# Letting ScalarE issue some of the loads of a gated linear attention kernel, with a new order of all its steps

## The chip, the cores and the metric

The kernel runs on one NeuronCore of a Trainium2 chip. The core has five engines, each with its own queue of instructions that it works through in order: TensorE (PE, matrix products), VectorE (DVE), ScalarE (ACT), GpSimd (POOL) and SyncE (SP, which here only issues DMA transfers). Sixteen DMA engines move data between the device's memory and the core. The engines meet only through semaphores. The metric is the device time of one execution in microseconds (us).

## The reference

Gated linear attention for 4 batches, 8 heads, 768 tokens and 48 features a head, then a feed-forward layer with the greatest of three projections. In the reference's words, cut to what matters:

```python
state = np.zeros((B, H, D, D))
for t in range(S):
    state = alpha[:, :, t, :, None] * state + np.einsum('bhd,bhe->bhde', k[:, :, t], v[:, :, t])
    y[:, :, t] = np.einsum('bhd,bhde->bhe', q[:, :, t], state)
x = y.transpose(0, 2, 1, 3).reshape(B * S, H * D)          # 3072 x 384
h = np.maximum(np.maximum(x @ w1, x @ w2), x @ w3)         # 3072 x 768
out = h @ w_out                                            # 3072 x 384
```

All arrays come and go as 32-bit floats; inside, the kernel uses 16-bit floats for what TensorE reads.

## The kernel before, in words

**Tiling.** The 768 tokens are cut into six chunks of 128. A *unit* u is one chunk of one batch: 24 units, numbered chunk by chunk, u = 4 x chunk + batch. Two units of one chunk make a *group* n (12 groups), for which alpha, q, k and v are loaded together. Each of the four tensors has four buffers for groups (`LOADED = 4`), so group n reuses the buffer of group n - 4 and must wait until its readers are through. The first four groups are loaded in two halves of 192 KB a tensor (each half is one unit), the others in one piece of 384 KB. The weights come in eight pieces between them.

**The steps of a unit**, with the engine and the line of the profile in brackets. `load` brings alpha, q, k, v (SP, line 304). `ln` takes the logarithm of alpha (ACT, 398), `totals` and `e` turn it into the decay over half a chunk (PE 408, ACT 414), `G` into the decay of a whole one (DVE 420). `cums` sums the logarithms over the tokens with a triangular matrix (PE 438); `ep` and `en` are its exponentials, up and down (ACT 443, 446); `q~` and `k~` are q and k scaled by them (DVE or POOL, 450), `v` is v scaled and rounded (POOL or ACT, 457, 460). `turn` transposes q~ and k~ by eight matmuls with an identity (PE 479) and `qkT` copies the result out of PSUM (DVE or ACT, 486); for eight of the late units a DMA transpose, `cross`, does both (SP, 469). `scores` multiplies them (PE 495), `LA` applies the causal mask on the way out (DVE 500), `outs` multiplies with v and with the state Z of the earlier chunks (PE 538, 541), `xb` brings the result to memory (ACT or DVE, 552, 554), `x turn` and `xT` transpose it (PE 568; DVE or ACT 573), or `cross x` does for three units (SP, 561). `sums`, `U` and `Z` carry the state to the next chunk (PE 600, DVE 607, POOL or DVE 613).

**The feed-forward layer.** max(x w1, x w2, x w3) is written as x w1 + max(relu(x (w2 - w1)), x (w3 - w1)). So `cast` rounds w1 and w_out (ACT 329), `sub` builds the two differences (DVE or POOL, 337), and `w1 turn`, `w1T`, `fold`, `w1o` multiply w1 by w_out once (PE 362, 379; ACT 368, 386). For one unit or two at a time, `grow` forms the two products (PE 638), `relu` (ACT 649) and `max` (DVE 654) combine them, `shrink` multiplies by w_out and adds x times w1o (PE 674), `ob` copies the result out (ACT or DVE, 689) and `store` writes it (ACT or SP, 694). 27 `zeros` matmuls without use (PE 582) keep TensorE occupied at the start. `clear` (POOL 345) zeroes the padding of buffers that are used again.

**What sets the order.** The 801 steps are built in a list, each with its readers and writers; then one loop issues them in the order of the tuple `ORDER`, on the engine that the dictionary `PICK` chooses from the step's options (the first where it names none), with the PSUM banks of the tuple `BANKS`. All three are written out by hand as numbers; nothing is decided at run time:

```python
for i in ORDER:
    how, _, run, deps, _, _ = self.steps[i]
    done.add(i)
    run(how[PICK.get(i, 0)][0])
```

The numbers in the options are the costs that a planner used and have no effect here. As every engine's queue is in order, a step that waits holds what stands behind it on its engine. In the built program all DMAs share eight completion counters in turn, whichever engine issues them, and an issue waits, where it must, until the earlier DMA on its counter has landed.

Before, all 64 loads, the eight pieces of weights, eleven DMA transposes and seven stores are issued by SP; ACT issues two constants and 18 stores.

Of the kernel before, what the change touches and what calls it, by code (L numbers as in the profile page):

```python
# [32 lines left out]


ORDER = (
# [44 lines left out]
)  # L80
BANKS = (
# [9 lines left out]
)  # L91
PICK = {
# [8 lines left out]
}  # L101

HARD, HARD_LOAD, HARD_LATE, LATE_FROM = 0.5, 1.8, 1.5, 3


def load_options(share, n):
    return [("SP", HARD, 0, HARD_LOAD * share, HARD_LATE * (n >= LATE_FROM))]  # L110


def weight_options(share, cast):
# [57 lines left out]
def kernel(  # L171
# [125 lines left out]
    def load(n):  # L297
        cb, g = divmod(n, B // UB)
        pieces = [(i * H, (i + 1) * H) for i in range(UB)] if n < HALF_LOADS else [(0, HG)]
        for lo, hi in pieces:  # L300
            for x in "akqv":
                t = ld[x][n % LOADED]
                plan.step(f"load {x} {n} {lo}", load_options((hi - lo) / HG, n), n,
                          lambda e, x=x, t=t, lo=lo, hi=hi: engines[e].dma_start(  # L304
                              t[:, lo:hi],
                              views[x][cb * P:(cb + 1) * P, g * HG + lo:g * HG + hi]),
                          writes=[(x, n % LOADED, h) for h in range(lo // H, hi // H)])
# [455 lines left out]
```

## Time and profile before

| | before |
|---|---|
| median of three runs | 155.6 us |
| runs | 155.11, 155.60, 156.13 us |
| span of the profiled execution | 466.5 us |
| busy in it: PE, DVE, ACT, POOL | 457.5, 112.5, 90.1, 48.0 us |
| first matmul starts | 4.32 us |
| last issue, a store by SP | 463.93 us |
| moved: read, written | 23.69 MB, 4.72 MB |

The profiled execution took three times as long as the timed runs, and has to be read with that in mind: TensorE's matmuls in it are slow, the other engines wait for them, and so its idle times, its chain of waits and the moments at which things happen after the first few microseconds are not those of the timed runs. The durations of single instructions on the other engines, the sizes of transfers and the order of instructions are what can be used.

In a row of the view of groups stand line, engine, operation, output and input with partitions and elements, the count, busy time in all (us), the mean of one (ns), and the idle time of the engine before them with what ended it. In a timeline row the first number is the start, the second the duration; engines with a q (SPq, ACTq) are DMA issues on that engine's queue.

### The profile page before, as it was taken

Reading aid. Unit: us, or ns where it says so; the run is one execution under the profiler, and the core shown is the slowest. Engines: PE = TensorE matmul, PEld = TensorE weight load, DVE = VectorE, ACT = ScalarE, POOL = GpSimd, SP = SyncE. Lnnn points to the kernel's source line nnn. Section 1 sums busy time; section 2 is a strip of 40 time slices with the busy share of each in tenths; the row PEclk is TensorE's granted clock in tenths of the full one; section 3 lists DMA queues with packets and bytes.
Section 4 is the critical chain, followed back from the end, with each engine's and each line's share of the span. In section 5 each row is a group of like instructions: output and inputs, shape, how many; then the busy total and the mean of one; then the engine's idle time right before and its main releaser. Section 6 shows DMA issues by size and latency. Waiting matters only on the chain.

```text
span 466.5 us, 4171 instructions
## 1 busy us (share of the span) xinstructions
PE 457.5 (98%) x1683; PEld 263.5 (56%) x1683; DVE 112.5 (24%) x196; ACT 90.1 (19%) x177; POOL 48.0 (10%) x72
## 2 busy tenths in 40 slices
PE   4999999999999999999999999999999999999997
PEld 1667556674555656547546645545546554567473
DVE  5420313131123122222412221322221321231100
ACT  4323221122121312111212200121220111001010
POOL 0110002003001030210111120011110020000000
DMA  9999500540087000700032640020550030100001
GB/s 179 272 287 209 110 0 1 111 76 1 0 163 124 1 0 18 152 17 35 0 60 49 141 91 9 2 62 0 112 112 17 18 79 25 35 0 25 1 34 34
DMA packets 116131, 31.07 MB, mean 67 GB/s; under 512 B 109712, under 2 KB 114960, under 8 KB 116112
## 3 DMA queue, kind: packets, MB, share of 16 engines
q1 hardware_dynamic: 113232, 27.27, 27.9%
q10 hardware_dynamic: 2880, 3.54, 2.2%
q8 instruction: 13, 0.21, 0.2%
q14 instruction: 6, 0.05, 0.0%
HBM read 23.69 MB, written 4.72 MB: 61 GB/s over the span
## 4 chain that ended last, share of the span: by engine, by line
PE 98%; DMA 1%; SPq 0%; DVE 0%; issue 0%; DVEq 0%
PE psum L638 38%; PE psum L674 29%; PE psum L479 6%; PE psum L495 4%; PE psum L582 4%; PE psum L541 3%; PE psum L438 3%; PE psum L568 3%; PE psum L600 3%; PE psum L538 2%; PE psum L379 2%; DMA qn<-in_q_dram 1%; PE psum L362 1%; PE psum L408 1%; SPq L304 0%; DVE qk L450 0%
## 5 line engine op out<-in xcount | busy, mean ns | idle before, releaser
L638 PE MATMUL psum<-xT,wd 128*128 128x256 f16 (+1 forms) x540 | 186.4, 602 | 0.0
L638 PEld LDWEIGHTS <-wd 128*128 128x128 f16 x540 | 105.1, 209 | 67.5 <-issue 61.5
L674 PE MATMUL psum<-wo,hT 128*128 128x384 f16 (+1 forms) x150 | 96.7, 887 | 0.0
L674 PEld LDWEIGHTS <-hT 128*128 128x128 f16 x150 | 34.4, 230 | 54.6 <-issue 52.0
L674 PE MATMUL psum<-w1o,xT 128*128 128x384 f16 (+1 forms) x75 | 50.1, 847 | 0.0
L654 DVE TENSOR_TENSOR hT<-psum,hT 128x512 f16<-128x512 f32 (+1 forms) x39 | 24.7, 647 | 99.7 <-PE psum L638 99.7
L649 ACT ACTIVATE hT<-psum 128x512 f16<-128x512 f32 (+1 forms) x39 | 21.7, 564 | 111.0 <-PE psum L638 111.0
L500 DVE TENSOR_TENSOR LA<-psum,c 128x1024 f16<-128x1024 f32 x24 | 28.9, 1221 | 41.0 <-PE psum L495 28.7
L541 PE MATMUL psum<-v,LA 128*128 128x48 f16 x192 | 30.3, 314 | 0.0
L541 PEld LDWEIGHTS <-LA 128*128 128x128 f16 x192 | 26.5, 179 | 5.7 <-issue 5.1
L613 POOL TENSOR_TENSOR Z<-U,G 48x192 f16<-48x192 f32 x26 | 14.1, 543 | 109.5 <-DVE U L607 108.5
L438 PE MATMUL psum<-la,c 128*128 128x384 f16 x24 | 19.9, 847 | 4.3 <-ACT la L398 4.3
L479 PE MATMUL psum<-c,qk 128*128 128x128 f16 x96 | 22.1, 480 | 1.7 <-DVE qk L450 1.7
L479 PEld LDWEIGHTS <-qk 128*128 128x128 f16 x96 | 16.9, 208 | 9.1 <-DVE qk L450 4.0
L450 POOL TENSOR_TENSOR qk<-qn,ep 128x384 f16<-128x384 f32 x11 | 10.9, 994 | 105.2 <-ACT ep L443 94.0
L674 PEld LDWEIGHTS <-xT 128*128 128x128 f16 x75 | 13.1, 185 | 14.7 <-issue 14.2
L582 PE MATMUL psum<-Z 128*128 128x384 f16 x27 | 20.2, 869 | 0.0
L443 ACT ACTIVATE ep<-psum 128x384 f32<-128x384 f32 x24 | 11.7, 494 | 41.3 <-PE psum L438 41.2
L689 ACT COPY ob<-psum 128x384 f32<-128x384 f32 (+1 forms) x18 | 8.3, 469 | 54.7 <-PE psum L674 54.7
L554 DVE TENSOR_SCALAR xb<-psum,c 128x384 f16<-128x384 f32 x15 | 9.2, 617 | 37.9 <-PE psum L541 37.9
L568 PE MATMUL psum<-c,xb 128*128 128x128 f16 x63 | 17.5, 455 | 0.0
L446 ACT ACTIVATE en<-psum 128x384 f32<-128x384 f32 x24 | 11.5, 490 | 28.4 <-PE psum L438 27.1
(61 smaller groups left out, 297.2 us busy)
## 6 DMA issues: line engine op xcount, KB each, us to landing
out_dram<-ob ACTq DMA_DIRECT2D x17, 192.0 KB, 1.9
an<-in_alpha_dram SPq DMA_DIRECT2D x8, 384.0 KB, 5.3
kn<-in_k_dram SPq DMA_DIRECT2D x8, 384.0 KB, 5.4
qn<-in_q_dram SPq DMA_DIRECT2D x8, 384.0 KB, 5.7
vn<-in_v_dram SPq DMA_DIRECT2D x8, 384.0 KB, 4.2
ws<-in_moe_w_dram SPq DMA_DIRECT2D x3, 768.0 KB, 6.7
an<-in_alpha_dram SPq DMA_DIRECT2D x8, 192.0 KB, 4.0
kn<-in_k_dram SPq DMA_DIRECT2D x8, 192.0 KB, 4.0
```

The costliest lines, as they stand in the source:

```text
L438: nc.tensor.matmul(live[Lk], tri, la[:, hs, :D], start=True, stop=True)
L479: nc.tensor.transpose(live[tk][:, w, j, :], qk[:, w, 2 * j:2 * j + 2, :], ident)
L495: nc.tensor.matmul(live[Ak][:, p, j * P:(j + 1) * P], qkT[rows, 1, j, :], qkT[rows, 0, j, :], start=True, stop=True)
L500: lambda e: nc.vector.tensor_mul(LA.rearrange("p a b t -> p (a b) t"), live[Ak].rearrange("p a (b t) -> p (a b) t", t=P), maskA.unsqueeze( ...
L541: nc.tensor.matmul(yp[:, 2 * j + p, :], LA[:, p, j, :], v16[:, 2 * j + p, :], start=(cb == 0), stop=True, skip_group_check=True)
L568: nc.tensor.transpose(live[xk][:, ft, :], xb[:, ft * P:(ft + 1) * P], ident)
L582: nc.tensor.matmul(live["wm"], zero[:, :P], zero, start=True, stop=True)
L613: lambda e, rows=rows, cols=cols: engines[e].tensor_mul(Zn[rows, :, cols], (Us[u % 3] if cb else live[pk])[rows, :, cols], G[rows, i * NP: ...
L638: nc.tensor.matmul(live[gk][:, jj, :], wd[:, kt, g, j * P:(j + 1) * P], xT[:, kt, :], start=(kt == 0), stop=(kt == NFT - 1))
L649: lambda e, h=h, gk=gk: nc.scalar.activation(out=h, in_=live[gk], func=AFT.Relu),
L654: lambda e, h=h, gk=gk: nc.vector.tensor_max(h, live[gk], h),
L674: nc.tensor.matmul(live[ok][:, cols], a[:, i * P:(i + 1) * P], w[:, cols], start=(kt == 0), stop=(kt == nk - 1))
```

## The change

`load_options` gets a second option, ACT, and the three tables of numbers are new. The core of the diff:

```diff
 def load_options(share, n):
-    return [("SP", HARD, 0, HARD_LOAD * share, HARD_LATE * (n >= LATE_FROM))]
+    return [("SP", HARD, 0, HARD_LOAD * share, HARD_LATE * (n >= LATE_FROM)), ("ACT", 0.45, 0, HARD_LOAD * share)]
 ORDER = (
-    4, 5, 6, 0, 8, 9, 65, 2, 82, 1, 83, 84, 85, 10, 86, 64, 34, 88, 123, 3, 92, 89, 68, 7, 127,
...
+    0, 14, 12, 8, 5, 4, 123, 2, 64, 124, 13, 6, 1, 125, 9, 34, 3, 10, 65, 66, 82, 68, 127, 84,
...
 PICK = {
-    44: 1, 71: 1, 72: 1, 75: 1, 79: 1, 81: 1, 85: 1, 86: 1, 120: 1, 131: 1, 132: 1, 145: 1, 146:
...
+    2: 1, 17: 1, 18: 1, 19: 1, 20: 1, 23: 1, 27: 1, 29: 1, 31: 1, 45: 1, 81: 1, 122: 1, 130: 1,
...
```

The steps and their number are the same, 1683 matmuls among them. What the tables make of them, step by step with the engine that runs it:

| step | before | after |
|---|---|---|
| load | SP 64 | SP 41, ACT 23 |
| q~ and k~ | DVE 25, POOL 23 | DVE 17, POOL 31 |
| v | POOL 14, ACT 10 | POOL 13, ACT 11 |
| qkT | DVE 9, ACT 7 | DVE 15, ACT 1 |
| xb | DVE 15, ACT 9 | DVE 9, ACT 15 |
| xT | DVE 14, ACT 7 | DVE 6, ACT 15 |
| Z | POOL 26, DVE 14 | POOL 23, DVE 17 |
| ob | ACT 18, DVE 7 | ACT 12, DVE 13 |
| store | ACT 18, SP 7 | ACT 17, SP 8 |

The 23 loads on ACT are eight of q, three of alpha, three of k and nine of v, spread from the eighth place of `ORDER` to the 681st; ten of them are among the first 45 DMAs. In the built program 20 of the 23 wait for an earlier DMA on their counter.

At the start the order of the loads is another. Before, SP issues alpha, k and q of unit 1, then alpha of unit 0 and unit 2, and so on; unit 1 is through first. After, SP issues alpha of unit 0, q and alpha of unit 3, alpha of unit 2, k and alpha of unit 1, then k of unit 3 and q of unit 1; q of unit 0 is issued by ACT. k~ and q~ of units 1 and 0 are on POOL instead of DVE. The last piece of weights comes after 15 loads instead of 16.

120 rows, old and new, of tables (BANKS, ORDER, PICK) are left out of this document.

## The prediction

> **What bounds the kernel now.** I read the page first: the span, the busy times, the DMA queues, the chain that ended last.
>
> ```profile
> span 466.5 us, 4171 instructions
> ...
> PE 457.5 (98%) x1683; PEld 263.5 (56%) x1683; DVE 112.5 (24%) x196; ACT 90.1 (19%) x177; POOL 48.0 (10%) x72
> ...
> q1 hardware_dynamic: 113232, 27.27, 27.9%
> q10 hardware_dynamic: 2880, 3.54, 2.2%
> ...
> PE 98%; DMA 1%; SPq 0%; DVE 0%; issue 0%; DVEq 0%
> ```
>
> The profiled execution is not an execution like the timed ones. Its span is 466.5 us, the timed median 155.6 us, and its TensorE alone is busy for 457.5 us. So in the timed runs TensorE went at least 457.5 / 155.6 = 2.9 times as fast. The timeline of PE shows the slow pace directly:
>
> ```profile
> 7.90 0.95 PE L582 MATMUL psum<-Z 128*128 128x384 f16 x1
> ...
> 8.53 1.58 PE L438 MATMUL psum<-la,c 128*128 128x384 f16 x2
> ```
>
> One matmul of 384 columns shows 0.95 us, two show 1.58, so the second came 0.63 us after the first. The Trainium skill ("TensorE: Matmul & The Clock Gate", section "What's actually happening") gives 2.4 GHz for a warm array, which would be 0.16 us for 384 columns; its caveat in "Seeing it yourself", a clock stuck at a quarter for 50 us and more, agrees with the 0.63 us here, although this profile puts the granted clock at 1.000. By that figure PE's work would be, as an estimate, 457.5 x 0.16 / 0.63 = 116 us of the 155.6.
>
> The chain of waits (98% PE) therefore says nothing of the timed runs. What does hold there is what the other engines did, as their instructions do not run on PE's clock: VectorE 112.5 us, ScalarE 90.1, GpSimd 48.0; and the DMA engines' packets, (27.9% + 2.2%) of 466.5 = 140.4 us. Set against 155.6 us, DMA is at 90%, VectorE at 72%, ScalarE at 58%. PE's own share there is not in the trace. So the kernel has no single bound that I can name: it is a weave of four, each waiting for the others a little. The table by stretches shows where DMA is full:
>
> ```profile
> 0.00:20.00 20.00, 13.99 (x77) 7.64 (x78) 10.86 (x30) 8.46 (x13) 2.35 (x7) 1.00 0.93 216
> 20.00:40.00 20.00, 20.00 (x79) 12.25 (x77) 5.06 (x6) 5.72 (x11) 2.63 (x2) 1.00 1.08 267
> ```
>
> The last two columns are the DMA engines' share and GB/s: from the start to 40 us they are saturated, from SyncE's queue almost alone, and a piece of 192 KB takes 196.6 / 267 = 0.74 us there.
>
> I make my sum in differences on the rows of the side engines and set it on the median of 155.6 (155.11 to 156.13); the 466.5 us cannot carry it. About 1% (1.6 us) is what a measurement of this kernel can tell from no change.
>
> **The change, part by part.** *Side engines.* The work is the same; the steps are picked anew. Rows for the steps that change sides, in the view of groups by shape:
>
> ```profile
> L450 DVE TENSOR_TENSOR qk<-kn,en 128x384 f16<-128x384 f32 x11 | 6.4, 598 | 11.6 <-ACT en L446 11.6
> L450 POOL TENSOR_TENSOR qk<-qn,ep 128x384 f16<-128x384 f32 x11 | 10.9, 994 | 105.2 <-ACT ep L443 94.0 <-DMA qn<-in_q_dram 11.1
> ...
> L486 ACT COPY qkT<-psum 128x1024 f16<-128x1024 f16 x5 | 5.1, 1012 | 14.3 <-PE psum L479 14.3
> L486 DVE COPY qkT<-psum 128x1024 f16<-128x1024 f16 x6 | 4.2, 692 | 30.6 <-PE psum L479 30.6
> ...
> L689 ACT COPY ob<-psum 128x384 f32<-128x384 f32 x17 | 8.0, 478 | 48.7 <-PE psum L674 48.7
> L689 DVE COPY ob<-psum 128x384 f32<-128x384 f32 x6 | 3.2, 555 | 16.8 <-PE psum L674 16.8
> ...
> L573 DVE COPY xT<-psum 128x384 f16<-128x384 f16 x14 | 4.8, 356 | 38.9 <-PE psum L568 38.8
> L573 ACT COPY xT<-psum 128x384 f16<-128x384 f16 x7 | 3.3, 477 | 23.7 <-PE psum L568 23.7
> ...
> L554 DVE TENSOR_SCALAR xb<-psum,c 128x384 f16<-128x384 f32 x15 | 9.2, 617 | 37.9 <-PE psum L541 37.9
> L552 ACT ACTIVATE xb<-psum,c 128x384 f16<-128x384 f32 x9 | 5.2, 581 | 53.3 <-PE psum L541 53.3
> ...
> L457 ACT ACTIVATE v<-vn,c 128x384 f16<-128x384 f32 x10 | 6.2, 617 | 0.7 <-DMA vn<-in_v_dram 0.7
> L613 DVE TENSOR_TENSOR Z<-U,G 48x192 f16<-48x192 f32 x6 | 3.0, 493 | 0.1
> L613 POOL TENSOR_TENSOR Z<-U,G 48x192 f16<-48x192 f32 x26 | 14.1, 543 | 109.5 <-DVE U L607 108.5
> ```
>
> VectorE gives eight of q~ and k~ to GpSimd (-8 x 0.598 = -4.8), takes six qkT (+6 x 0.692 = +4.2) and six ob (+6 x 0.555 = +3.3) from ScalarE, gives it eight xT (-8 x 0.356 = -2.8) and six xb (-6 x 0.617 = -3.7), and takes three Z (+1.5): -2.4 in all (by the unrounded products), so 110.1 us. ScalarE: -6 x 1.012 - 6 x 0.478 + 8 x 0.477 + 6 x 0.581 + 0.617 for one v = -1.0. GpSimd: +8 x 0.994 - 3 x 0.543 = +6.3, so 54.3: far below the others, no cost.
>
> *Twenty-three loads on ScalarE.* An issue is not counted as busy, but it holds the engine that makes it, and what is queued behind it: ep and en (line 443, 446), which q~ and k~ wait for, relu, which frees the bank that PE's grow fills, and xb, xT, which PE's next transposes and grows wait for. The price is not in the trace, as ScalarE issues only constants and stores there. From below, its stores; from above, SyncE's issues of these very loads (min/median/max ns):
>
> ```profile
> L694 ACTq DMA_DIRECT2D out_dram<-ob x18: 338/338/446, 129.1 to 463.2; - x18
> ```
>
> ```profile
> L304 SPq DMA_DIRECT2D an<-in_alpha_dram x16: 457/847/3164, 0.7 to 327.4; - x16
> L304 SPq DMA_DIRECT2D kn<-in_k_dram x16: 507/1300/2517, 1.3 to 329.8; - x16
> L304 SPq DMA_DIRECT2D qn<-in_q_dram x16: 646/1309/1673, 1.9 to 328.1; - x16
> L304 SPq DMA_DIRECT2D vn<-in_v_dram x16: 368/878/3893, 9.4 to 341.2; - x16
> ```
>
> Moved are 8 loads of q, 3 of alpha, 3 of k, 9 of v. At SyncE's medians they cost 8 x 1.309 + 3 x 0.847 + 3 x 1.300 + 9 x 0.878 = 24.8 us; at its shortest, 0.368, a load with nothing ahead of it, 8.5 us. ScalarE's queue is emptier than SyncE's, but the DMA engines behind both are the same, so I take the middle between that shortest one and the longest median: 0.84 us, 19.3 us in all. That a load is not always cheap even behind an idle queue, these two pairs show, a store and the load right behind it, in the timeline of SyncE:
>
> ```profile
> 86.19 0.36 SPq L694 DMA_DIRECT2D out_dram<-ob  x1
> 86.60 1.18 SPq L304 DMA_DIRECT2D qn<-in_q_dram  x1
> ...
> 276.81 0.36 SPq L694 DMA_DIRECT2D out_dram<-ob  x1
> 277.21 0.43 SPq L304 DMA_DIRECT2D vn<-in_v_dram  x1
> ```
>
> The same pair costs 0.43 or 1.18 us; no view says what else the DMA engines had at 86.6. A packet of PE's instructions would be such a thing, and then loads issued when one comes get the dear price.
>
> So ScalarE, issues included: before 90.1 + 18 x 0.338 = 96.2; after 96.2 - 1.0 - 0.3 (one store less) + 19.3 = 114.2. It passes VectorE's 112.5, which has been the busiest engine beside PE and stands for the pace that the side engines allow. I cost the change at that difference, 114.2 - 112.5 = +1.7 us. Below 112.5, that is below (112.5 - 94.9) / 23 = 0.77 us an issue, this term is nothing.
>
> *Start.* Before, the three loads of one unit come first:
>
> ```profile
> 3.74 0.52 ACT L398 ACTIVATE la<-an 128x384 f16<-128x384 f32 x1 [0.83 <-DMA an<-in_alpha_dram]
> 4.32 0.53 PE L438 MATMUL psum<-la,c 128*128 128x384 f16 x1 [4.32 <-ACT la L398]
> ...
> 6.53 1.69 PE L479 MATMUL psum<-c,qk 128*128 128x128 f16 x8 [1.69 <-DVE qk L450]
> 6.74 0.52 ACT L398 ACTIVATE la<-an 128x384 f16<-128x384 f32 x1 [0.99 <-DMA an<-in_alpha_dram]
> 7.61 0.52 ACT L398 ACTIVATE la<-an 128x384 f16<-128x384 f32 x1 [0.35 <-DMA an<-in_alpha_dram]
> ```
>
> The first, fourth and fifth load let ln start at 3.74, 6.74 and 7.61. Afterwards unit 1 needs the sixth load on SyncE (about 8.5) and its k~ and q~ stand on GpSimd, one after the other at 0.994: the first transposes come at about 8.5 + (6.53 - 3.74) + 2 x (0.994 - 0.598) = 12.1 instead of 6.53, 5.6 us later. I cost it at nothing: until the last weight is in, PE has little else to do, and that comes after 15 loads instead of 16, 0.74 us sooner. The cover ends where the last weight lands, at about 32 us (4.3 MB by 20 us, the other 3.4 at 267 GB/s). Without it the cost is up to 5.6 us, with it the gain up to 0.7.
>
> *Order and banks* of the rest: no row prices them. PE's matmuls are the same 1683. Sum: 155.6 + 1.7 = 157.3 us.
>
> **The rivals.** *Faster, 153.2 us:* the issues are cheap. At under (110.1 - 94.9) / 23 = 0.66 us ScalarE stays below VectorE's new 110.1, and VectorE's own -2.4 us shows. For it: ScalarE's stores never took over 0.446 us; against it, SyncE's medians.
>
> *No change, 155.6 us:* DMA sets the pace, and who issues does not matter. For it: 0.93 and 1.08 of the DMA engines in the first 40 us, from one queue. The Trainium skill ("DMA: Bandwidth & Descriptors", section "Issuing engines are not separate DMA queues") has that rule: transfers of all engines run on the same sixteen and interleave, and a second issuer only saves the time of issuing; those two shares agree, and by it the time would stay.
>
> *Much slower, 164.7 us:* ScalarE is held by completion counters. In the built programs the DMAs share eight counters in turn, and an issue waits until the DMA eight places earlier has landed; 20 of the 23 loads carry such a wait. Landings:
>
> ```profile
> kn<-in_k_dram SPq DMA_DIRECT2D x8, 384.0 KB, 5.4
> kn<-in_k_dram SPq DMA_DIRECT2D x8, 192.0 KB, 4.0
> ```
>
> Eight pieces at 0.74 are 5.9 us, barely over a landing, so in the saturated stretch the counters come free just as they are wanted. Ten of the loads stand among the first 45 DMAs; held by one delivery each, they add 10 x 0.74 = 7.4 to ScalarE: 121.6, +9.1. It decides once the holds exceed what the engine waits for anyway.
>
> **How the numbers follow.** Slower by dear issues 0.43, faster 0.25, no change 0.20, held 0.12. The first case reaches from 155.6 to 162.7 (the medians, 94.9 + 24.8 = 119.7, +7.2); about 0.06 of its chance lies within 1%. So faster by over 1%: 0.25; within: 0.20 + 0.06, say 0.27; slower: 0.48. The likeliest case gives 157.3. The range goes from 152.5, the faster rival with the 0.7 of the start (153.2 - 0.7), to 163.0, the dear end of the first case; it leaves out the held case and, for the unpriced order, some of both ends.
>
> **What would show it.** In the profile after: load issues on ScalarE's queue with a median near 0.84 us (under 0.66: the faster rival; waits on DMA landings just before them: the held one); ScalarE's busy time at about 89 (90.1 - 1.0) and VectorE's at 110; the first transposes at about 12.1 us. The forecast is wrong if the issues are dear and the time does not rise, as ScalarE then had the room, or if the time moves by more than the side engines' sums do, as then the new order did it.

## The result, and the profile after

| | before | after |
|---|---|---|
| median | 155.36 us (4 runs, 154.19 to 156.13) | 160.03 us (4 runs, 158.69 to 160.07) |
| ratio, 95% interval | 1 | 1.0304 (1.0240 to 1.0368) |

The change makes the kernel 3% slower. The ratios are those to the kernel before in runs beside it; here and below they leave disturbed runs out, so they need not be the quotients of the medians. The profiled execution of the kernel before ran its TensorE at a quarter of the pace of the timed runs, so nothing can be set beside it; the kernel before was therefore profiled once more (156.37 us), and "before" below is that execution.

> The kernel before once more, for a profile in which TensorE runs at its normal pace, so that it can be laid beside the profile after. Expected time about 155.4 us (median of the four runs so far). Theory 'start' (the 4.7 us between the kernels arise in the first 45 us): PE is idle less than the 15 us or so that it is idle there after, and from then on the two kernels take equally long. Theory 'weave' (the new order costs all along): PE's idle time in the first 45 us is about the same in both, and the difference builds up afterwards.

From the pages, first of before, then of after: the span, the engines' busy time, for after the two DMA queues, and the chain of waits by engine (SPq and ACTq are the issues on the queues of SyncE and ScalarE).

```profile
span 154.6 us, 4171 instructions
...
PE 135.8 (88%) x1683; PEld 105.9 (69%) x1683; DVE 108.7 (70%) x196; ACT 88.1 (57%) x177; POOL 48.5 (31%) x72
...
PE 48%; SPq 25%; DMA 20%; issue 3%; ACT 1%; DVE 1%; POOL 0%; DVEq 0%; POOLq 0%; ACTq 0%
```

```profile
span 158.2 us, 4150 instructions
...
PE 136.4 (86%) x1683; PEld 106.1 (67%) x1683; DVE 107.4 (68%) x189; ACT 86.9 (55%) x180; POOL 56.4 (36%) x76
...
q1 hardware_dynamic: 75120, 20.19, 62.5%
q10 hardware_dynamic: 40992, 10.62, 32.7%
...
PE 73%; DMA 10%; SPq 7%; DVE 4%; issue 2%; ACT 1%; ACTq 0%; DVEq 0%
```

TensorE is the busiest of the engines in both, at 135.8 and 136.4 us; what changed is its idle time, 154.6 - 135.8 = 18.8 us before and 158.2 - 136.4 = 21.8 after. Before, the chain of waits runs through TensorE for only 48% of the span and through SyncE's issues and transfers for 45%; after, for 73% and 17%. VectorE and ScalarE lost 1.3 and 1.2 us of work, and no gain in time shows. Where the idle time lies, the table by stretches tells. It gives for PE, PEld (TensorE's loading of weights), DVE, ACT and POOL the busy time and the number of instructions, then the granted clock (the share of its full clock that TensorE was given), the DMA engines' share, and GB/s. Before:

```profile
0.00:10.00 10.00, 3.51 (x21) 1.61 (x21) 5.21 (x24) 5.36 (x10) 0.20 (x4) 1.00 0.87 172
10.00:20.00 10.00, 7.57 (x75) 5.13 (x76) 6.26 (x8) 3.50 (x4) 2.14 (x3) 1.00 0.90 236
20.00:30.00 10.00, 9.23 (x114) 7.17 (x112) 3.66 (x6) 7.57 (x15) 2.60 (x2) 1.00 1.08 330
30.00:40.00 10.00, 9.48 (x129) 7.46 (x128) 8.73 (x14) 6.74 (x17) 2.45 (x4) 1.00 1.00 208
```

After:

```profile
0.00:10.00 10.00, 1.22 (x18) 0.87 (x19) 3.37 (x20) 3.21 (x5) 0.20 (x4) 1.00 0.91 180
10.00:20.00 10.00, 8.22 (x62) 4.52 (x60) 4.31 (x6) 5.57 (x12) 5.44 (x6) 1.00 1.05 256
20.00:30.00 10.00, 7.33 (x106) 5.01 (x104) 6.85 (x8) 5.22 (x9) 4.24 (x3) 1.00 1.10 347
30.00:40.00 10.00, 6.39 (x48) 5.20 (x48) 2.63 (x2) 3.62 (x7) 0.56 (x2) 0.66 0.91 175
```

By 40 us TensorE has done 21 + 75 + 114 + 129 = 339 matmuls before, but 18 + 62 + 106 + 48 = 234 after, with 29.8 and 23.2 us of work: 6.6 us more idle time. Only 3.0 us of that is left at the end, so after 40 us TensorE idles 3.6 us less than before. That the new order is the better one there is not shown: the loads can have got ahead while TensorE stood still, and without the pause that follows here the new order is no faster than the old (`late_ln` below). The last stretch also shows a granted clock of 0.66. What happened between 22 and 40 us, the timeline of after shows (start, duration, what; in brackets the idle time before it and what ended it):

```profile
22.31 0.39 ACTq L304 DMA_DIRECT2D an<-in_alpha_dram  x1
...
26.06 0.80 ACT L368 COPY w1T<-psum 128x768 f16<-128x768 f16 x1
...
27.50 1.18 PE L638 MATMUL psum<-xT,wd 128*128 128x128 f16 x18 [0.46 <-POOL wd L337]
...
30.93 2.63 DVE L337 TENSOR_TENSOR wd<-ws,w1h 128x1536 f16<-128x1536 f32 x2 [2.63 <-DMA ws<-in_moe_w_dram]
...
32.67 0.52 ACT L398 ACTIVATE la<-an 128x384 f16<-128x384 f32 x1 [5.81 <-DMA an<-in_alpha_dram]
...
33.10 0.46 ACT L573 COPY xT<-psum 128x384 f16<-128x384 f16 x1
...
33.61 1.12 PE L638 MATMUL psum<-xT,wd 128*128 128x128 f16 x9 [4.94 <-ACT xT L573]
...
34.84 3.09 PE L638 MATMUL psum<-xT,wd 128*128 128x128 f16 x27
```

ScalarE has nothing wrong with its work; it stands still. After the w1T copy its next instruction is `ln 2 1`, the logarithm of alpha for unit 5, whose load was issued at 22.31 and lands at 32.65. For 5.81 us ScalarE waits for it, and everything behind it on its in-order queue waits too: the xT copy of unit 2, the first relu, the cast of w_out that the fold needs. TensorE runs out of work at 28.7 and stands for 4.94 us. The matmuls behind the pause run at half pace: 27 of 128 columns take 3.09 us, 0.114 each, where 36 of them take 2.17 us, 0.060 each, in a kernel without the pause (below). The last two pieces of the weights, which VectorE turns into wd from 30.93 to 33.56, come in just as late; so the held queue did not so much delay the next matmul as take away what TensorE would have done meanwhile. In the trace of before, no ln made ScalarE wait over 2.05 us; the two of units 4 and 5, at 34.30 and 35.70, stand behind six relus:

```profile
22.95 0.52 ACT L398 ACTIVATE la<-an 128x384 f16<-128x384 f32 x1 [2.05 <-DMA an<-in_alpha_dram]
...
34.30 0.52 ACT L398 ACTIVATE la<-an 128x384 f16<-128x384 f32 x1 [0.21 <-DMA an<-in_alpha_dram]
...
35.70 0.52 ACT L398 ACTIVATE la<-an 128x384 f16<-128x384 f32 x1 [0.52 <-DMA an<-in_alpha_dram]
```

What the prediction had looked for, the issues of loads on ScalarE, came out cheap. By line and queue (durations min/median/max in ns, then first and last start):

```profile
L304 ACTq DMA_DIRECT2D vn<-in_v_dram x9: 374/375/1672, 43.7 to 126.1; - x9
...
L304 ACTq DMA_DIRECT2D qn<-in_q_dram x8: 374/398/456, 6.7 to 118.5; - x8
...
L304 ACTq DMA_DIRECT2D an<-in_alpha_dram x3: 374/385/397, 22.3 to 77.5; - x3
L304 ACTq DMA_DIRECT2D kn<-in_k_dram x3: 374/374/397, 39.4 to 106.0; - x3
```

Twenty-three at the medians are 8.8 us, not 19.3. Nor did they hold ScalarE: in this trace each of them runs while ScalarE works on instructions that were ahead of it, and none of its idle time falls into any of the 23. For example:

```profile
39.40 0.48 ACT L386 CAST w1o<-psum 128x384 f16<-128x384 f32 x1 [3.70 <-PE psum L379]
39.41 0.37 ACTq L304 DMA_DIRECT2D kn<-in_k_dram  x1
39.77 1.26 ACT L649 ACTIVATE hT<-psum 128x384 f16<-128x384 f32 x3
```

The issue is over before the cast is, and the relus follow at once. During the longest issue, 1.67 us from 43.72, ScalarE started four further instructions that stood ahead of it.

### The profile page after: what moved, and what is told of

Same layout as the page of the kernel before. It is cut to its first block, busy times and chain, and to the rows that moved or that the text cites. A ratio compares the mean times of both kernels' runs of the same rounds, so it can differ in the third digit from the quotient of the medians.

```text
span 158.2 us, 4150 instructions
## 1 busy us (share of the span) xinstructions
PE 136.4 (86%) x1683; PEld 106.1 (67%) x1683; DVE 107.4 (68%) x189; ACT 86.9 (55%) x180; POOL 56.4 (36%) x76
## 4 chain that ended last, share of the span: by engine, by line
PE 73%; DMA 10%; SPq 7%; DVE 4%; issue 2%; ACT 1%; ACTq 0%; DVEq 0%
PE psum L638 31%; PE psum L674 21%; DMA an<-in_alpha_dram 7%; SPq L304 6%; PE psum L495 4%; DMA qn<-in_q_dram 4%; PE psum L479 4%; PE psum L438 2%; PE psum L541 2%; PE psum L538 2%; PE psum L379 2%; PE psum L600 2%; PE psum L568 2%; DVE LA L500 1%; DVE qk L450 1%
## 5 line engine op out<-in xcount | busy, mean ns | idle before, releaser
L638 PE MATMUL psum<-xT,wd 128*128 128x256 f16 (+1 forms) x540 | 55.5, 258 | 5.4 <-ACT xT L573 4.9
L638 PEld LDWEIGHTS <-wd 128*128 128x128 f16 x540 | 44.7, 101 | 11.2 <-issue 5.2
L500 DVE TENSOR_TENSOR LA<-psum,c 128x1024 f16<-128x1024 f32 x24 | 28.7, 1218 | 2.7 <-PE psum L495 1.8
L674 PE MATMUL psum<-wo,hT 128*128 128x384 f16 (+1 forms) x150 | 27.5, 320 | 0.0
L450 POOL TENSOR_TENSOR qk<-kn,en 128x384 f16<-128x384 f32 x12 | 12.5, 1041 | 23.5 <-ACT en L446 21.9
L674 PEld LDWEIGHTS <-hT 128*128 128x128 f16 x150 | 14.5, 98 | 8.9
L398 ACT ACTIVATE la<-an 128x384 f16<-128x384 f32 (+1 forms) x16 | 10.8, 684 | 10.3 <-DMA an<-in_alpha_dram 10.3
L674 PE MATMUL psum<-w1o,xT 128*128 128x384 f16 (+1 forms) x75 | 15.8, 320 | 0.0
L450 POOL TENSOR_TENSOR qk<-qn,ep 128x384 f16<-128x384 f32 x10 | 10.3, 1028 | 12.8 <-ACT ep L443 7.3
L552 ACT ACTIVATE xb<-psum,c 128x384 f16<-128x384 f32 x15 | 8.5, 583 | 5.5 <-PE psum L541 5.5
L541 PE MATMUL psum<-v,LA 128*128 128x48 f16 x192 | 10.9, 184 | 0.0
L479 PE MATMUL psum<-c,qk 128*128 128x128 f16 x96 | 8.2, 235 | 2.4 <-POOL qk L450 1.8
```

Of the source, the lines that this page charges most:

```text
L450: lambda e, w=w, x=x, d=d: engines[e].tensor_mul(qk[:, w, :, :D], ld[x][n % LOADED][:, hs], d),
L479: nc.tensor.transpose(live[tk][:, w, j, :], qk[:, w, 2 * j:2 * j + 2, :], ident)
L500: lambda e: nc.vector.tensor_mul(LA.rearrange("p a b t -> p (a b) t"), live[Ak].rearrange("p a (b t) -> p (a b) t", t=P), maskA.unsqueeze( ...
L541: nc.tensor.matmul(yp[:, 2 * j + p, :], LA[:, p, j, :], v16[:, 2 * j + p, :], start=(cb == 0), stop=True, skip_group_check=True)
L638: nc.tensor.matmul(live[gk][:, jj, :], wd[:, kt, g, j * P:(j + 1) * P], xT[:, kt, :], start=(kt == 0), stop=(kt == NFT - 1))
L674: nc.tensor.matmul(live[ok][:, cols], a[:, i * P:(i + 1) * P], w[:, cols], start=(kt == 0), stop=(kt == nk - 1))
```

## The experiments

Three theories stood at the start: the loads on ScalarE cost the time; the late start of unit 1 costs it; ScalarE held behind one late load costs it, in two parts, the wait itself and the slow clock behind it. (The expectations call `ln 2 1` the ln of unit 3; it is that of unit 5, the second of group 2.)

**All loads back on SyncE.** The kernel after, with the 23 entries of loads struck from `PICK`; order, banks and the other engines stay.

```diff
 PICK = {
-    2: 1, 17: 1, 18: 1, 19: 1, 20: 1, 23: 1, 27: 1, 29: 1, 31: 1, ...
+    ...
```

> The changed kernel with all 23 loads issued by SyncE again, each at its place of the new order; all else as changed. Theory 'dear issues' (my forecast's step: the issues hold ScalarE): the time falls to within 1% of before, 155 to 157 us. Theory 'start order' (what costs is the order at the start, where ln of unit 3's alpha stands ahead of xT on ScalarE and waits for a load): it stays at 159 to 161 us, as the load is not earlier on SyncE's queue. Theory 'two queues help' (ScalarE's issues are cheap and pass SyncE's waits): it gets slower than 161 us.

Measured: 159.8 us (159.18 to 161.46, 4 runs), ratio to before 1.0352 (1.0243 to 1.0461). No time is seen to come back. ScalarE is held at the same place, and the clock falls there too (timeline, in which ln stands at line 396, then the table by stretches):

```profile
33.42 0.52 ACT L396 ACTIVATE la<-an 128x384 f16<-128x384 f32 x1 [6.01 <-DMA an<-in_alpha_dram]
```

```profile
30.00:40.00 10.00, 5.64 (x50) 4.65 (x50) 2.63 (x2) 3.93 (x8) 0.56 (x2) 0.83 1.03 202
```

So who issues the loads is not what costs the 3%. The slow clock was shorter here: 0.83 over 10 us is 3.4 us at half the clock, the 0.66 of after is 6.8 us. Yet the kernel is not seen to be faster for it.

**One order joined to the other.** Four kernels put the start of one order before the rest of the other.

```
start_before    first 173 steps of before, the rest in the order of after
start_after     first 166 steps of after, the rest in the order of before
start_before2   first 208 steps of before, the rest in the order of after
start_after2    first 208 steps of after, the rest in the order of before
```

In the first two, one PSUM bank is used by two steps at once at the seam, so that part of the products is overwritten; the amount of work is the whole one.

> The first 173 steps in the order, and with the engines and banks, of before (to the first shrink), all others in the order of after; 18 loads stay on ScalarE. Theory 'start': the loss is gone, 154 to 156 us. Theory 'weave': it stays at 158 to 160 us.

> The first 166 steps as in after (to the first shrink), all others in the order of before; 5 loads on ScalarE. Theory 'start': the whole loss is here, 159 to 161 us. Theory 'weave': 155 to 156.5 us.

> The first 208 steps (to LA 4, PE's first 44 us or so) in order, engines and banks of before, all others as in after; 16 loads stay on ScalarE. Unlike the earlier kernel of this kind, no PSUM bank is used twice at the seam. Theory 'start': the loss is gone, and as PE idles less after 40 us in the changed kernel (4.9 us against 8.6), the time is below before: 152 to 155 us. Theory 'weave': 157 us or more.

> The counterpart: the first 208 steps (to v 5) as in after, all others as in before; 7 loads on ScalarE. Theory 'start': 159 to 163 us, that is, the loss of the start without the gain of the rest. Theory 'weave': 155 to 156.5 us.

Measured: start_before 157.13 us (154.49 to 157.46, 4 runs, too wide for an interval), between its two expectations, so it decides nothing; start_after 160.63, ratio 1.0327 (1.0152 to 1.0502); start_after2 163.61, ratio 1.0596 (1.0526 to 1.0667). With the start of after the loss is there in both, and start_after2, whose ScalarE waits 5.73 us for the same load, loses even more; why more, was not traced. But the reverse failed: start_before2 took 158.78 us, ratio 1.0231 (1.0144 to 1.0317), where 'start' had 152 to 155 and 'weave' 157 or more. Its chain of waits shows one reason (start, duration):

```profile
39.33 5.22 DMA an<-in_alpha_dram
...
44.95 0.84 ACT la L398
...
46.22 0.34 PE psum L408 x8
```

At the seam an ln again stands on ScalarE ahead of a relu, and waits for its alpha: the hybrid has a hold of its own. Joining orders is a poor experiment here, as a seam makes new waits; whether all of the loss lies in the start, it leaves open.

**The one step.** The kernel after with two steps moved: `ln 2 1` (156) to just before `ln 2 0` (155), and `cums 5` (180), which reads it, behind `cums 4` (166).

```diff
 ORDER = (
-    ... 118, 53, 156, 44, ... 277, 293, 180, 21, ... 61, 284, 155, ... 280, 166, 157,
+    ... 118, 53, 44, ... 277, 293, 21, ... 61, 284, 156, 155, ... 280, 166, 180, 157,
```

> The changed kernel with two steps moved: ln of unit 3 of group 2 (ln 2 1) from before xT 2 to just before ln 2 0 on ScalarE, and its cums 5 to just behind cums 4 on TensorE. Theory 'held ScalarE' (ScalarE waits 5.8 us for the load behind that ln, PE 4.9 us behind xT 2, and the clock falls for some 7 us after): PE no longer stops at 28.7 us, no slow clock, and of the 4.7 us 3 or more come back: 155 to 157 us. Theory 'start order of the loads' (what is late is everything, since alpha, k and q of unit 1 come as fifth, sixth and eighth): PE stops elsewhere before 45 us, and it stays at 158.5 to 160 us.

Measured: 155.53 us (153.56 to 155.82, 10 runs), ratio 1.0046 (0.9992 to 1.0101). Of the 3.04% that the change costs, 2.58%, or 4.0 us, come back when one `ln` moves on ScalarE's queue and its reader follows on TensorE's. The timeline and the table by stretches:

```profile
28.57 2.18 PE L638 MATMUL psum<-xT,wd 128*128 128x128 f16 x36 [0.32 <-DVE wd L337]
...
30.59 3.09 PE L379 MATMUL psum<-wo,w1T 128*128 128x384 f16 x18
...
33.51 2.17 PE L638 MATMUL psum<-xT,wd 128*128 128x128 f16 x36
...
34.46 0.95 ACT L398 ACTIVATE la<-an 128x384 f16<-128x384 f32 x2
```

```profile
20.00:30.00 10.00, 8.21 (x127) 6.22 (x126) 7.05 (x8) 7.94 (x13) 4.24 (x3) 1.00 1.09 349
30.00:40.00 10.00, 9.68 (x112) 7.11 (x109) 7.12 (x11) 6.64 (x17) 2.78 (x5) 1.00 1.12 209
```

The two logarithms now run at 34.46 without a wait in front, and where the pause of 4.94 us was, TensorE does 36 matmuls and the fold (18 matmuls of line 379). The weights are no earlier: VectorE is through with their last two pieces at 33.72, so it was not they that made the pause. The clock stays at 1.00. The DMA engines are as full as before (349 GB/s), and loads still take up to 11.0 us to land; only nobody on ScalarE needs this one yet.

**The wait or the clock.** The kernel after, hold and all, but TensorE is given 30 matmuls without use in the pause:

```diff
+        def pause(e):
+            for _ in range(30):
+                zeros(e)
+
         for i in range(count):
-            plan.step(f"zeros {i}", [("PE", 0.163)], 90.0, zeros,
+            plan.step(f"zeros {i}", [("PE", 0.163)], 90.0, pause if i == 26 else zeros,
```

and `zeros 26` (118) stands just before `grow 0 0 0` (277).

> The kernel after, with ScalarE's wait left in place, but PE is given work in it: the last of the zeros steps is moved behind the 18 matmuls that precede the pause and issues 30 matmuls of 384 columns instead of one (0.16 us each, 4.9 us in all; they add nothing to the result). Theory 'the pause costs twice, once as a wait of 4.9 us and again as a slower clock behind it': the wait stays, the granted clock of 30 to 40 us goes from 0.66 to 1.00, and that part of the loss (about 3 us: 234 matmuls done by 40 us instead of some 290) comes back: 156.5 to 158. Rival 'the clock follows something else, or what it loses is hidden behind ScalarE and VectorE anyway': the time stays at 159.5 to 160.5, or rises by the 4.9 us of matmuls that push on: up to 161.

Measured: 158.3 us (157.38 to 158.87, 4 runs), ratio 1.0237 (1.0172 to 1.0302). Timeline and stretch:

```profile
28.30 5.04 PE L582 MATMUL psum<-Z 128*128 128x384 f16 x30
...
33.46 0.52 ACT L398 ACTIVATE la<-an 128x384 f16<-128x384 f32 x1 [6.01 <-DMA an<-in_alpha_dram]
...
36.68 3.09 PE L379 MATMUL psum<-wo,w1T 128*128 128x384 f16 x18
```

```profile
30.00:40.00 10.00, 8.94 (x84) 6.14 (x83) 2.63 (x2) 4.86 (x10) 0.56 (x2) 1.00 0.95 184
```

The hold is as long as ever (6.01 us), and the clock is 1.00 instead of 0.66: a TensorE kept busy keeps its clock. The time lies between the two expectations, nearer to that of the clock: the ratio falls by 0.67%, about 1.0 us, and the two intervals overlap. So the clock's part, some 1.0 of the 4.0 us by these figures, is not told from nothing, and its size stays open; the larger part of the loss is the lost work of the wait, as far as the figures go.

**Who issues, once the hold is gone.** The kernel of the one step, with all loads on SyncE.

```
late_ln_sp   ORDER and BANKS of late_ln, no load in PICK
```

> The kernel after with the two moved steps (ln 2 1 and cums 5 later, 155.5 us) and all 23 loads back on SyncE. Theory 'who issues does not matter, at 0.4 us an issue': 155 to 156, the same as with the loads on ScalarE. Rival 'the loads on ScalarE were worth something that the held ScalarE hid': 157 to 158.5, as SyncE's loads come later, each behind the one before. Rival 'the waits of ScalarE's loads cost': below 154.5.

Measured: 156.52 us (154.09 to 159.02, 12 runs), ratio 1.0096 (1.0031 to 1.0160), beside 1.0046 (0.9992 to 1.0101) with the loads on ScalarE. The intervals overlap: 0.5% may be what ScalarE's issuing is worth, or nothing.

**The same loads on ScalarE in the kernel before.** Its own order, banks and engines, with ScalarE as the second option of a load and the same 23 loads picked for it.

```diff
 def load_options(share, n):
-    return [("SP", HARD, 0, HARD_LOAD * share, HARD_LATE * (n >= LATE_FROM))]
+    return [("SP", HARD, 0, HARD_LOAD * share, HARD_LATE * (n >= LATE_FROM)), ("ACT", 0.45, 0, HARD_LOAD * share)]
```

> The kernel before, order and engines unchanged, but the same 23 loads issued by ScalarE, each at its place of the old order. Theory 'issues are cheap' (0.37 to 0.4 us each, about 9 us of ScalarE's idle time): within 1% of before, 154 to 157 us. Theory 'dear issues': the forecast's 19 us on ScalarE, and 1 to 5 us in the time, 157 to 160 us.

Measured: 161.09 us (158.9 to 163.1, 4 runs), too wide for an interval, yet all above the 17 runs of before beside it (153.21 to 156.95). The issues are as cheap as in after (medians 374 to 408 ns), and still it is slower. The chain of waits:

```profile
58.19 8.44 DMA kn<-in_k_dram
66.65 0.38 ACTq L304
67.12 0.61 ACT hT L649
67.77 0.34 PE psum L408 x8
```

Here a load of alpha on ScalarE cannot be issued before an earlier load of k has landed: the two share one completion counter. It stands some 2.5 us at the head of ScalarE's queue (the instruction before it ends at 64.1), with a relu behind it, and TensorE waits for that relu. A shorter hold of this kind, 0.87 us, ends at 44.97. Whether such holds make up the whole loss is not shown. In the profile of after no issue on ScalarE is held that way.

**The late start.** The kernel of the one step with unit 1 first again: its loads of alpha, k and q lead, and q~ and k~ of unit 1 go from POOL back to DVE. Nine banks are set anew.

```diff
 ORDER = (
-    0, 14, 12, 8, 5, 4, 123, 2, 64, 124, 13, 6, 1, 125, ...
+    (load a 0 8, load k 0 8, load q 0 8, ln 0 1, load a 0 0, load a 1 0,
+     cums 1, en 1, ep 1, q~ 1, k~ 1, turn 1, then the rest as it was)
```

> The kernel after with the two moved steps, and with unit 1 first again, as before the change: its three loads come first, and its k and q products go back from GpSimd to VectorE; the rest keeps its order, with nine PSUM banks set anew so that none is used twice. Theory of the prediction 'the late start is covered until the last weight is in': the first transposes at 6.5 to 8 us instead of 12.8 and the time within 1% of 155.5. Rival 'the late start costs on the path': 152 to 154, by part of the 5.6 us. If it is slower than 156.5, the order that follows does not suit the loads' new order.

Measured: 153.92 us (152.73 to 154.46, 12 runs), ratio 0.9979 (0.9944 to 1.0014). The first transposes in after, and here:

```profile
12.78 1.04 PE L479 MATMUL psum<-c,qk 128*128 128x128 f16 x8 [1.78 <-POOL qk L450]
```

```profile
6.52 1.08 PE L479 MATMUL psum<-c,qk 128*128 128x128 f16 x8 [1.57 <-DVE qk L450]
```

6.3 us earlier for unit 1 bring 0.67%, some 1.0 us, against the kernel of the one step, by intervals that just overlap. So the start is covered for the most part, and that the rest of it costs anything is not clear of the noise. By its ratio this is the fastest of the changed kernels, 3.2% faster than after; against before its interval takes in 1, so it is not shown to beat it.

**The miss looked at again.** start_before2 with the ln that made its own hold (`ln 4 0`) moved behind the relu, to just before `totals 4`.

```
start_before2   ... LA 4, zeros 26, ln 4 0, grow 3 0 0, max 2 1, relu 3 0, grow 3 0 1, ln 3 1, ... totals 4
start_before3   ... LA 4, zeros 26, grow 3 0 0, max 2 1, relu 3 0, grow 3 0 1, ln 3 1, ... ln 4 0, totals 4
```

> The kernel start_before2 (the first 208 steps in the order of before, the rest as after, 158.8 us) with one step moved: ln 4 0, which at 44.95 us held ScalarE and the relu behind it until its alpha had landed, now stands behind that relu and the ln of unit 7, just before the totals that read it. Theory 'its loss was a second hold of the same kind, made at the seam': the pause of PE at 44 us goes and the time falls by 2 to 3.5 us, to 155.3 to 156.8. Rival 'the two orders do not fit together in more places than that': it stays at 158 to 159.

Measured: 155.27 us beside 153.0 for before on the same chip, ratio 1.0138 (1.0068 to 1.0209), beside 1.0231 (1.0144 to 1.0317): 1.4 us back, less than expected, with intervals that overlap. The relu no longer waits and the clock is 1.00 there, but TensorE still waits, now for the ln itself:

```profile
45.24 0.35 PE L408 MATMUL psum<-c,la 128*128 128x2 f16 x8 [1.68 <-ACT la L398]
```

Its alpha is loaded too late for the order that follows. The rest of that kernel's 1.4% was not traced.

## Why the prediction was right in sign and wrong in its cause

The forecast of 157.3 us, with 152.5 to 163.0 around it, was on the right side, and 160.03 lies within. That is luck: its +1.7 us came from a term that is nothing in the trace, and the loss lies in a term that it put at nothing.

*What bounds the kernel.* The estimate of 116 us for TensorE was too low: it is busy for 135.8 us of 154.6 in a normal execution. That no single engine bounds the kernel before held, with a chain of 48% TensorE, 25% SyncE's issues and 20% transfers; but the engine whose pauses lengthen the run is TensorE and not VectorE, at 108.7 us. From this the next step went wrong.

*Side engines.* The sums were near: VectorE forecast 2.4 us down, measured 1.3; ScalarE 1.0 and 1.2; GpSimd 6.3 up, measured 7.9 (the sum left out that GpSimd also gives one v away). That the busiest engine beside PE "stands for the pace that the side engines allow" was an error: no run shows VectorE's saving in the time.

*Twenty-three loads on ScalarE.* This is the term of the sum that failed, in size and in kind. The price taken was 0.84 us, the middle of two bounds; measured are medians of 0.374 to 0.398, the low bound. By the prediction's own point, 0.77 us, the term is then nothing, not +1.7. And an issue did not hold "the engine that makes it": all 23 in after run beside ScalarE's own work, so their time is not to be added to its busy time. What holds ScalarE is a wait at the head of its queue, an issue's in before_act, an ln's in after. SyncE's medians were a poor upper bound; that its queue is fuller is a likely reason, not a tested one. after_sp shows the same from the other side: without these issues the time does not fall.

*Start.* Forecast for the first transposes 12.1 us, measured 12.78; costed at nothing, measured at about 1.0 of the possible 5.6, not clear of the noise. VectorE could take up the last two pieces of the weights at 30.93, where 32 was forecast for the end of the cover.

*Order and banks.* This term was put at nothing, as "no row prices them", and 4.0 of the 4.7 us lie in it. What the diff and the built program did show is that `ln 2 1` stands on ScalarE ahead of `xT 2`, the relus and a cast, and that its load is the 17th of the loads, in the stretch where the DMA engines are full. Following each load of alpha to the ln that waits for it, and reading what stands behind that ln, would have pointed at it; the landing time was the unknown, 10.3 us where the rows had medians of about 4.

*The rivals.* "Faster" had the right price of an issue and the wrong time, as VectorE's saving did not show in it. "No change" had a rule that held where it was tested: the Trainium skill ("DMA: Bandwidth & Descriptors", section "Issuing engines are not separate DMA queues") says that a second issuer saves only the time of issuing, and after and after_sp, 1.0304 and 1.0352, agree; the time did not stay, because the order changed as well. "Held by completion counters" was the nearest in kind: ScalarE held at the head of its queue by a landing. In after it is not the counter of an issue but the data of an ln that holds it, for 5.8 us in one place and not for 0.74 in ten; in before_act it is the counter indeed.

*What would show it.* The last sign named, that the time moves by more than the side engines' sums do and "the new order did it", is the one that came in.

## What to carry to other kernels

In an order written out by hand, the place of a step that waits for a transfer is a price by itself: for each load, find its first reader, and read what stands behind that reader on its in-order queue. Move the reader behind all that does not need it; two numbers moved in a list of 801 gave back 4 us of 4.7 here. And before pricing an edit by the busy time of side engines, make sure that one of them is the bound, with a profile at the pace of the timed runs, and see in the timeline whether what you add holds the engine or runs beside its work.

## What the runs showed of the hardware

The clock follows TensorE's own activity. Behind a pause of 4.94 us the granted clock was 0.66 over 10 us and matmuls took 0.114 us instead of 0.060; with 30 matmuls in the pause it was 1.00. The Trainium skill ("TensorE: Matmul & The Clock Gate", section "What's actually happening") says that one idle window of about 3.4 us halves the clock; the pause of after agrees, and in late_ln, which has no such pause there, the clock stays whole. But less than a whole such window was enough elsewhere: behind a pause of 2.20 us in start_before2 the granted clock was 0.90 and 0.92 in the two stretches from 40 to 60 us, and behind one of 1.96 us in before_act 0.92 and 0.91 from 60 to 80. Behind 1.68 us in start_before3, and behind another of 2.19 us in before_act, it stayed 1.00. So the length of a pause alone does not decide it in these runs.

The granted clock of the table is not to be trusted in the first 20 us, where it reads 1.00. Matmuls of 384 columns then, and later in the same execution of before:

```profile
20.35 0.81 PE L582 MATMUL psum<-Z 128*128 128x384 f16 x2
...
28.44 0.81 PE L582 MATMUL psum<-Z 128*128 128x384 f16 x4
```

Two take as long as four do later: the slow pace, which before keeps to about 22 us, while after is at the quick one by 18.4.

A load in the saturated stretch took far longer than the medians of before had shown, on either queue: 10.3 us for the 192 KB of unit 5's alpha in after on ScalarE's queue and 8.8 us in after_sp on SyncE's, where the eight pieces of this kind had a median of 4.1 us before. Before, the very same piece, issued at 28.31, took 7.4 us: a median over all stretches hides this. By groups and queue (KB each, median us to landing), after and then before:

```profile
an<-in_alpha_dram ACTq DMA_DIRECT2D x1, 192.0 KB, 10.3
```

```profile
an<-in_alpha_dram SPq DMA_DIRECT2D x8, 192.0 KB, 4.1
```
